# The down projection of one block pair as a Strassen level, summed in DRAM

## The chip, the cores and the metric

One core of a Trainium2 chip runs the whole kernel. The metric is the time of one execution on the device, in microseconds (us); of several runs the median counts.

## The reference

A transformer block on 2048 tokens of width D = 576, in float32: attention, then a gated feed-forward layer with F = 4608 hidden columns. Only the second half is touched here:

```
h   = x + attention(layernorm(x)) @ wo
n   = layernorm(h)
g   = n @ w_gate                  # 2048 x 4608
u   = n @ w_up
out = h + (sigmoid(g) * u) @ w_down   # w_down is 4608 x 576
```

## The kernel before

Tokens are split by parity and half into four blocks of 512 (`BLOCKS`), two to a pair: blocks 0 and 1 are pair 0, 2 and 3 pair 1. F is split into NF = 36 chunks of 128 hidden columns. The feed-forward part walks a list of items, one chunk for one block ("std") or for both blocks of a pair ("pair"):

```
items = ([("std", 0, f) for f in range(NSTD)] + [("pair", 0, f) for f in range(NSTD, NF)]
         + [("std", 1, f) for f in range(NSTD)] + [("pair", 1, f) for f in range(NF)])
```

While the first three runs of items go on, attention and output projection of later blocks run beside them (`bg_step`). The last run, 36 chunks of pair 1, has nothing beside it but its own down projection.

*Precision.* Each float32 operand of a matmul is split into a high part (ACT copies it into the format that TensorE reads) and a low part (DVE subtracts); this is `split`, lines L100 and L101. A product of two operands is then three matmuls: high x high, low x high, high x low.

*Gate and up* (`pair`). For a pair, gate and up are already one Strassen level over block, contraction half and gate/up: seven products `prod` (L532, six matmuls of 512 columns each), named b00, b10, t2, t3, t1, t4, b11 after their weights, and four small `rest` products (L539, two matmuls each) for the 64 left-over rows. That is 50 matmuls of 512 columns a chunk. They accumulate in three PSUM banks b1, b2, b3. ACT copies a running sum out of b1 between products (L588, L598, L605), DVE adds banks to these copies (L593, L606, L612), ACT takes the sigmoid, and DVE multiplies and splits the hidden tiles h0 and h1 (`hidden`, L545). Between the products stand the calls `side(i)`, i = 0 to 6, for background work.

*Weights.* SP loads chunk c + 2 (`load_gu`, L497: gate, up and down weights in one tile wg, two buffers) while chunk c is computed; `weights` forms the differences and splits, among them the 576 down columns into tile d.

*Down projection* (`down_units`). After every two chunks (a segment) one generator per block is put on a list, `queue`. Each of its four steps, called a unit, takes 128 tokens: 12 matmuls of 288 columns (L649: two chunks x three precision products x two column halves) into one of two PSUM tiles dp, then ACT copies 128x576 into the tile "stage" (L655). After the fourth unit POOL issues a DMA that adds the stage tile to the block's sum hacc[b] in DRAM (L659). `pair` calls `units(2)` at two places, after t1 and after b11, so two chunks give eight places for the eight units of a segment. hacc[b] was filled with h before. For blocks 2 and 3, the last two segments are added by DVE (L657) onto the sum read back by SP (L637), and SP writes the output (L663).

*Order.* The program is traced in this order, and a planner then orders each engine's instructions by priority (program order, with `high_priority` moving some ahead) and by the times that it expects: an instruction whose operands are not expected yet lets a later one go first. Each engine then runs its list strictly in order. Tiles of a pool share buffers; a new tile waits until all users of the old one are done.

Of the kernel before, what the change touches and what calls it, by code (L numbers as in the profile page):

```python
# [7 lines left out]

# [21 lines left out]
NS = 4  # L30
# [21 lines left out]
HI = 400  # L52
HC = 700
NSTD = 14


@with_exitstack
def kernel(ctx, tc, x, wqkv, wo, wmlp, out):
# [429 lines left out]
    st = ctx.enter_context(tc.tile_pool(name="st", bufs=2, reuse_waits="tile"))  # L488
# [6 lines left out]
    def load_gu(f, eng=sp):  # L495
        ws = gw.tile([P, WC], F32, bufs=2, name="wg")
        eng.dma_start(ws, wmlp[f])  # L497
        return ws

    def weights(kind, f, ws):  # L500
        with tc.high_priority(HI):
            wd = ws[:, GU:WC]
            r = ws[:, :GU].rearrange("p (c n) -> p c n", c=10)
            w1 = gw.tile([P, 2, 5, P], F32R, bufs=2, name="w1")
            split(w1[:, 0], w1[:, 1], r[:, 5:10])
            w4 = gw.tile([P, 2, 3, P], F32R, name="w4")
            w2 = gw.tile([P, 2, 4, P], F32R, name="w2")
            w3 = gw.tile([P, 8, P], F32R, name="w3").rearrange("p (a n) q -> p a n q", a=2)
            if kind == "std":
                split(w4[:, 0], w4[:, 1], r[:, 0:3])  # L510
                split(w2[:, 0, 0:2], w2[:, 1, 0:2], r[:, 3:5])
                ww = dict(b00=(w1, 0), b10=(w1, 2), b01=(w2, 0))
            else:
                t = gw.tile([P, 8, P], F32, name="tw")
                dve.tensor_tensor(t[:, 2:6], r[:, 1:5], r[:, 3:7], ALU.subtract)
                dve.tensor_tensor(t[:, 0:2], r[:, 1:3], t[:, 4:6], ALU.subtract)
# [6 lines left out]
        d = gd.tile([P, 2, D], F32R, bufs=4, name="d")  # L523
        split(d[:, 0], d[:, 1], wd)
        return ww, d

    def prod(ps, xx, w, n, first):
# [11 lines left out]
            pe.matmul(ps, wt[:, a, k0], xx[:, 4], start=False, stop=a == 1,  # L539
                      skip_group_check=True)  # L540

    def hidden(sg, ps, name):
        hh = gc.tile([P, TB], F32R, bufs=3, name=name + "h")
        hl = gc.tile([P, TB], F32R, bufs=3, name=name + "l")
        dve.tensor_tensor(sg, sg, ps, ALU.mult)  # L545
        split(hh, hl, sg)
        return hh, hl

    def s_tile():
        return gh.tile([P, TB], F32, tag="s", bufs=4, name="s")  # L550
# [29 lines left out]
        side(5)  # L580
        return {t: hid}

    def pair(X, w, units, side):
        b1, b2, b3 = b_tile(0), b_tile(1), b_tile(2)
        s1, s2, s3 = s_tile(), s_tile(), s_tile()
        prod(b1, X["a00"], w, "b00", True)
        with tc.high_priority(HC):
            act.activation(s1, b1, AF.Copy)  # L588
        side(0)
# [5 lines left out]
        side(1)  # L595
# [3 lines left out]
        side(2)  # L599
        prod(b3, X["s3"], w, "t3", True)  # L600
        side(3)
        prod(b1, X["s1"], w, "t1", False)
        rest(b1, X["a11"], w, "u4")
        with tc.high_priority(HC):
            act.activation(s3, b1, AF.Copy)  # L605
            dve.tensor_tensor(s3, s3, b3, ALU.add)  # L606
        units(2)
        side(4)
        prod(b3, X["a11"], w, "t4", False)
        rest(b3, X["a11"], w, "g4")  # L610
        with tc.high_priority(HC):
            dve.tensor_tensor(s2, s2, b3, ALU.add)  # L612
            act.activation(s2, s2, AF.Sigmoid)
        side(5)
        prod(b1, X["s4"], w, "b11", False)
        rest(b1, X["s4"], w, "u4")
        with tc.high_priority(HC):
            h0 = hidden(s1, b1, "h0")
            h1 = hidden(s2, s3, "h1")
        units(2)  # L620
        side(6)
        return {0: h0, 1: h1}

    tails = {}
    segs = [0] * 4
# [2 lines left out]
    def down_units(seg, b, t):  # L628
        e, hf = BLOCKS[b]
        left = NSEG - 1 - segs[b]  # L630
        segs[b] += 1
        add = b < 2 or left > 1
        if left != 0 or b < 2:
            hs = st.tile([P, NS, D], F32, name="stage")
            if not add:
                tails[b] = hs
                sp.dma_start(hs, hacc[b])  # L637
        else:
            hs = tails[b]
        for j in range(NS):  # L640
            js = slice(j * P, (j + 1) * P)
            ps = gp.tile([P, 2, 512], F32, bufs=2, name="dp")
            k = 0
            n = 3 * len(seg) - 1
            for hid, d in seg:
                hh, hl = hid[t]
                for a, m in ((hh, 0), (hl, 0), (hh, 1)):
                    for i in range(2):
                        pe.matmul(ps[:, i, :DH2], a[:, js], d[:, m, i * DH2:(i + 1) * DH2],  # L649
                                  start=k == 0, stop=k == n)  # L650
                    k += 1
            hv = hs[:, j].rearrange("p (i n) -> p i n", i=2)
            with tc.high_priority(HC):
                if add:
                    act.activation(hv, ps[:, :, :DH2], AF.Copy)  # L655
                else:
                    dve.tensor_tensor(hv, hv, ps[:, :, :DH2], ALU.add)  # L657
            if add and j == NS - 1:
                pool.dma_start(hacc[b], hs, accum_op=ALU.add, max_dma_last_dim=8 * D)  # L659
                if left == 0:  # L660
                    pool.dma_start(ov[e, hf], hacc[b])
            elif not add and left == 0:
                sp.dma_start(ov[e, hf][:, j], hs[:, j])  # L663
            yield


    def att_scr(at, blocks):
# [12 lines left out]
    def proj_scr(pj, b, raw, wos, wait):  # L680
# [10 lines left out]
        def tile_j(j, oj, hj):  # L691
            js = slice(j * P, (j + 1) * P)
            xj = []

            def put(pv, cs):
                if raw is None and not xj:
                    xj.append(pj.tile([P, 5, P], F32, bufs=2, name="xj"))
                act.activation(xj[0][:, cs] if raw is None else raw[:, cs, js], pv, AF.Copy)

            yield from proj_j(lambda: gp.tile([P, 512], F32, name="bgp"), oj, hj, wos,  # L700
                              th[:, :, js], tl[:, :, js], lambda: oj, put)
            act.dma_start(hacc[b][:, j], hj)
            if raw is None:
                act.dma_start(xscr[b][:, :, js], xj[0])

# [49 lines left out]
            yield from operands(pp, 0, X, ("s2", "s3", "s1", "a11", "s4"), a1)  # L755

    Xn = {}
    c = 0

    def under_rest(last_x):  # L760
# [18 lines left out]
        pp = ctx.enter_context(sb_pool("pp2", "right"))  # L779
        raw = yield from operands(pp, 1, Xn, ("s2", "s3", "s4"), a0)  # L780
        yield raw

# [40 lines left out]
    with tc.high_priority(2 * HI):  # L823
        wg = load_gu(0, pool)
        wg2 = load_gu(1, pool)
        wc = weights("std", 0, wg)
    wg = wg2
    seg = []

    def last_pair(i):  # L830
# [4 lines left out]
                X["a10"] = x_half(a10, None)  # L835
        bg_step(i)

    for c, (kind, p, f) in enumerate(items):
        w, d = wc
        skip = () if kind == "std" else (3,)  # L840
        if c == NSTD:
            finish_bg()
            last_x = splits[-1]
            bg = under_rest(getattr(last_x, "ins", last_x))
        if c == NF + NSTD:
            finish_bg()
            with tc.high_priority(HI):
                for n in ("s1", "a11"):
                    Xn[n] = x_half(*raw[n])
            X = Xn  # L850
        if c + 1 < len(items):
            wc = weights(items[c + 1][0], items[c + 1][2], wg)
        if c + 2 < len(items):
            wg = load_gu(items[c + 2][2])
        if kind == "std":
            hid = single(X, w, p, late, bg_step)
            blocks = [p]
        else:
            hid = pair(X, w, units, last_pair if c == NF - 1 else bg_step)
            blocks = [2 * p, 2 * p + 1]  # L860
        seg.append((hid, d))
        if len(seg) == 2:
            for b in blocks:
                queue.append(down_units(seg, b, b % 2))
            seg = []
# [44 lines left out]
```

## Time and profile before

| what | value |
|---|---|
| median of 3 runs | 1664.49 us (1664.44 to 1666.2) |
| profiled execution, its own time | 1665.37 us |
| its span in the profile | 1663.6 us, granted TensorE clock 0.981 |
| PE / DVE / ACT / POOL busy in the span | 96% / 68% / 49% / 6% |

PE is TensorE, PEld its loading of stationary operands, DVE VectorE, ACT ScalarE, POOL GpSimd, SP the engine that only issues DMAs. A group's row names the line of the code, the engine, the operation, out<-in with the names of tiles, the shape and the count; then busy us, mean ns, and idle time ahead with what ended it. A row of the timeline has start, duration, engine, line. Durations of matmuls overlap: their rate is read from starts.

### The profile page before, as it was taken

The numbers are of one execution on the slowest core, as the hardware profiler recorded it, in microseconds if no ns is written. First come the engines' busy times: TensorE is split into PE (matmuls) and PEld (weight loads), VectorE is DVE, ScalarE is ACT, GpSimd is POOL, SyncE is SP. The second block draws the span as 40 slices with busy tenths as digits, with TensorE's granted clock in tenths as the row PEclk, the third lists the DMA queues.
The fourth block names the chain that finished last, engine by engine and source line by source line (L and its number), as shares of the span: only waits on it lengthen the run. The fifth ranks groups of instructions, "written<-read, shape, count | busy, mean of one in ns | idle before, by whom it ended". The sixth has DMA issues, their size and how long they took to land.

```text
span 1663.6 us, 22174 instructions
## 1 busy us (share of the span) xinstructions
PE 1591.8 (96%) x8724; PEld 1416.3 (85%) x8724; DVE 1138.6 (68%) x1743; ACT 813.3 (49%) x1407; POOL 105.1 (6%) x114
## 2 busy tenths in 40 slices
PE   7899777999899999999899998999999999999999
PEld 6899776798788888888788897888888888888888
DVE  7999999456899999999444448644544545545544
ACT  5422224435555656655443446555555555555551
POOL 2000010000000000000000000000000000000000
PEclk9999988999999999999999999999999999999999
DMA  7447544757466676575957556365554455554562
GB/s 258 152 166 240 200 143 165 232 147 227 122 162 173 158 178 162 135 192 142 279 135 197 144 155 174 98 137 121 126 132 103 106 140 115 130 128 103 113 150 86
DMA packets 72392, 258.92 MB, mean 156 GB/s; under 512 B 8160, under 2 KB 20704, under 8 KB 71008
## 3 DMA queue, kind: packets, MB, share of 16 engines
q0 software_dynamic: 19328, 84.48, 26.8%
q1 hardware_dynamic: 32912, 143.60, 26.1%
q10 hardware_dynamic: 20048, 29.43, 4.8%
q8 instruction: 68, 1.11, 0.3%
q14 instruction: 36, 0.29, 0.1%
HBM read 145.42 MB, written 114.42 MB: 156 GB/s over the span
## 4 chain that ended last, share of the span: by engine, by line
PE 78%; DVE 9%; DMA 8%; ACT 2%; issue 1%; SPq 0%; POOL 0%; ACTq 0%; POOLq 0%; DVEq 0%
PE b L532 36%; PE dp L649 23%; PE acc L146 7%; PE b L539 7%; DMA wg<-in_wmlp_dram 5%; PE bgp L146 2%; DVE w L101 1%; DVE pr L194 1%; DMA o<-kw 1%; DVE pr L168 1%; DVE pr L199 1%; DVE lg L171 1%; DVE s L545 1%; PE acc L148 1%; PE acc L149 1%
## 5 line engine op out<-in xcount | busy, mean ns | idle before, releaser
L532 PE MATMUL b<-tl,w 128*128 128x512 f32 x1728 | 431.7, 395 | 18.0 <-ACT w L100 8.9
L532 PEld LDWEIGHTS b<-tl,w 128*128 128x128 f32 x1728 | 320.3, 190 | 82.3 <-ACT w L100 9.3
L532 PE MATMUL b<-th,w 128*128 128x512 f32 x1380 | 358.7, 395 | 4.4 <-DVE s L545 3.7
L532 PEld LDWEIGHTS b<-th,w 128*128 128x128 f32 x1380 | 256.0, 189 | 56.8 <-DVE s L545 4.0
L655 ACT ACTIVATE stage<-dp 128x576 f32<-128x576 f32 x272 | 175.9, 647 | 132.0 <-PE dp L649 128.7
L649 PE MATMUL dp<-d,h0h 128*128 128x288 f32 x1152 | 214.5, 297 | 4.9 <-ACT stage L655 4.9
L649 PE MATMUL dp<-d,h1h 128*128 128x288 f32 x1152 | 213.8, 296 | 0.0
L649 PEld LDWEIGHTS dp<-d,h0h 128*128 128x128 f32 x1152 | 179.5, 190 | 11.1 <-ACT stage L655 5.1
L649 PEld LDWEIGHTS dp<-d,h1h 128*128 128x128 f32 x1152 | 178.2, 189 | 5.6
L101 DVE TENSOR_TENSOR w<-wg,w 128x384 fp32r<-128x384 f32 (+2 forms) x200 | 129.0, 650 | 78.3 <-ACT w L100 78.2
L539 PE MATMUL b<-th,w 128*128 128x512 f32 x576 | 179.4, 393 | 0.0
L100 ACT ACTIVATE w<-wg 128x384 fp32r<-128x384 f32 (+2 forms) x200 | 117.8, 595 | 124.6 <-DMA wg<-in_wmlp_dram 50.9
L659 POOL DMA_DIRECT2D h<-stage x68 | 81.2, 1193 | 1189.4 <-ACT stage L655 1109.7
L146 PE MATMUL acc<-qw,th 128*128 128x432 f32 x512 | 155.9, 365 | 0.0
L101 DVE TENSOR_TENSOR w<-tw,w 128x512 fp32r<-128x512 f32 x116 | 79.8, 688 | 89.9 <-ACT w L100 89.7
L539 PEld LDWEIGHTS b<-th,w 128*128 128x128 f32 x576 | 109.4, 190 | 23.0
L612 DVE TENSOR_TENSOR s<-s,b 128x512 f32<-128x512 f32 x58 | 39.7, 685 | 126.2 <-PE b L539 126.2
L649 PE MATMUL dp<-d,h0l 128*128 128x288 f32 x576 | 124.9, 298 | 0.1
L649 PE MATMUL dp<-d,h1l 128*128 128x288 f32 x576 | 124.3, 297 | 0.0
L100 ACT ACTIVATE w<-tw 128x512 fp32r<-128x512 f32 x116 | 73.2, 631 | 88.5 <-PE b L532 84.6
L146 PEld LDWEIGHTS acc<-qw,th 128*128 128x128 f32 x512 | 98.5, 192 | 4.8 <-ACT th L100 0.3
L649 PEld LDWEIGHTS dp<-d,h0l 128*128 128x128 f32 x576 | 93.4, 190 | 0.6 <-DVE h0l L101 0.4
(185 smaller groups left out, 2075.1 us busy)
## 6 DMA issues: line engine op xcount, KB each, us to landing
h<-stage POOLq DMA_DIRECT2D x68, 1152.0 KB, 11.2
wg<-in_wmlp_dram SPq DMA_DIRECT2D x84, 928.0 KB, 5.4
kw<-k SPq DMA_DIRECT2D x16, 792.0 KB, 4.3
vw<-v SPq DMA_DIRECT2D x16, 792.0 KB, 4.6
h<-in_x_dram SPq DMA_DIRECT2D x20, 288.0 KB, 4.4
q<-ev ACTq DMA_DIRECT2D x16, 288.0 KB, 2.3
k<-ev ACTq DMA_DIRECT2D x16, 288.0 KB, 3.1
q<-q SPq DMA_DIRECT2D x16, 288.0 KB, 2.8
```

The costliest lines, as they stand in the source:

```text
L100: act.activation(hi, src, AF.Copy)
L101: splits.append(dve.tensor_tensor(lo, src, f32(hi), ALU.subtract))
L146: pe.matmul(ps[:, :n], a[:, c, js], m[:, c], start=k == 0, stop=False)
L148: pe.matmul(ps[:, :n], th[:, 4, js], wh[:, 4], start=False, stop=False)
L149: return pe.matmul(ps[:, :n], th[:, 4, js], wl[:, 4], start=False, stop=True)
L168: dve.tensor_tensor(pr[:, i], kw[:, j:j + W], q[:, j].unsqueeze(1).broadcast_to([P, W, CG]), ALU.mult)
L532: pe.matmul(ps, wt[:, a, k0 + c], xx[:, m + c], start=first and k == 0, stop=k == 5, skip_group_check=True)
L539: pe.matmul(ps, wt[:, a, k0], xx[:, 4], start=False, stop=a == 1, skip_group_check=True)
L612: dve.tensor_tensor(s2, s2, b3, ALU.add)
L649: pe.matmul(ps[:, i, :DH2], a[:, js], d[:, m, i * DH2:(i + 1) * DH2], start=k == 0, stop=k == n)
L655: act.activation(hv, ps[:, :, :DH2], AF.Copy)
L659: pool.dma_start(hacc[b], hs, accum_op=ALU.add, max_dma_last_dim=8 * D)
```

## The change

For the first 32 chunks of pair 1, the down projection takes two chunks (f even and odd), two blocks and two column halves of 288 as the three factors of a 2 x 2 x 2 product and does it as seven products instead of eight, in the form with running sums: hidden sums s1 to s4 (`seven`) and weight differences t1 to t4 (`down_side`). In detail:

- `down_seven` has 14 units: for each half u of 256 tokens, seven products k = 0 to 6 of six matmuls of 288 columns. Even products accumulate in one PSUM tile px, products 1 and then 3, 5 in py. After each, ACT copies the running sum to a tile "ev"; for every two products POOL adds it to one of seven sums in DRAM, `hsev`, that replaces hacc[2] and hacc[3].
- `pair` calls `between(i)` at seven places; in pair 1 each place takes one unit (in pair 0 two units at places 4 and 6, as before). Two chunks have 14 places.
- Down weights of pair 1 are loaded by themselves, two chunks at once (`load_down`), and split in `down_side`.
- A generator `lag(3)` puts three empty places ahead of the first `seven`.
- The residual h of blocks 2 and 3 is written to rows 0, 6, 2 and 4 of hsev; rows 1, 3 and 5 are filled with zeros by a memset tile z and two DMAs.
- The last NPL = 4 chunks stay with `down_units`. Ahead of them `load_tails` reads all seven sums back, adds three of them by DVE, and leaves five empty places.

```diff
-    hacc = [dr.tile([P, NS, D], F32, name=f"h{b}") for b in range(4)]
+    hacc = [dr.tile([P, NS, D], F32, name=f"h{b}") for b in range(2)]
+    hsev = dr.tile([P, 2, 7, 2, DH2], F32, name="h7")
...
+    def down_seven(ops):
+        for u in range(2):
+            for k, (a, m) in enumerate(ops):
+                if k == 0:
+                    px = gp.tile([P, 2, 512], F32, bufs=2, name="dp")
+                elif k in (1, 3):
+                    py = gp.tile([P, 2, 512], F32, bufs=2, name="dp")
+                ps = px if k % 2 == 0 else py
+                for i in range(2):
+                    js = slice((2 * u + i) * P, (2 * u + i + 1) * P)
+                    for q, (x, y) in enumerate(((0, 0), (1, 0), (0, 1))):
+                        pe.matmul(ps[:, i, :DH2], a[x][:, js], m[y],
+                                  start=k in (0, 1, 3) and q == 0, stop=q == 2,
+                                  skip_group_check=True)
+                if k % 2 == 0:
+                    hs = st.tile([P, 2, 2, DH2], F32, bufs=4, name="ev")
+                with tc.high_priority(HC):
+                    act.activation(hs[:, k % 2], ps[:, :, :DH2], AF.Copy)
+                if k % 2 or k == 6:
+                    k0 = k - k % 2
+                    pool.dma_start(hsev[:, u, k0:k + 1], hs[:, :k + 1 - k0], accum_op=ALU.add,
+                                   max_dma_last_dim=8 * D)
+                yield
...
+    def down_side(f, i):
+        if f % 2 == 0 and i == 0:
+            load_down(f)
+        t = M["wd"].rearrange("p c (h n) -> p c h n", h=2)
+        with tc.high_priority(HI):
...
+            elif f % 2:
+                if i == 0:
+                    d = dw.tile([P, 2, DH2], F32R, bufs=2, name="d3")
+                    split(d[:, 0], d[:, 1], t[:, 1, 1])
+                    M["b11"] = d[:, 0], d[:, 1]
+                    M["b00"], M["b10"] = pair_d(t[:, :, 0])
+                elif i == 4:
+                    dve.tensor_tensor(t[:, 0, 0], t[:, 0, 1], t[:, 0, 0], ALU.subtract)
+                    dve.tensor_tensor(t[:, 0, 1], t[:, 1, 1], t[:, 0, 1], ALU.subtract)
+                    dve.tensor_tensor(t[:, 1, 1], t[:, 1, 1], t[:, 0, 0], ALU.subtract)
+                    dve.tensor_tensor(t[:, 1, 0], t[:, 1, 0], t[:, 1, 1], ALU.subtract)
+                    M["t3"], M["t2"] = pair_d(t[:, :, 1])
+                elif i == 6:
+                    M["t1"], M["t4"] = pair_d(t[:, :, 0])
...
+    def seven():
+        r00, r01, r10, r11 = (R[n] for n in ("00", "01", "10", "11"))
+        sx = dk.tile([P, TB], F32, name="sx")
+        with tc.high_priority(HI):
+            dve.tensor_tensor(sx, r10, r11, ALU.add)
+            dve.tensor_tensor(r10, r00, r10, ALU.subtract)
+            dve.tensor_tensor(r00, sx, r00, ALU.subtract)
+            s2 = sum_halves("s2", r00)
+            s3 = sum_halves("s3", r10)
+            s1 = sum_halves("s1", sx)
+            a11 = halves("h1", r11)
+            dve.tensor_tensor(r01, r01, r00, ALU.subtract)
+            s4 = sum_halves("s4", r01)
+        return down_seven(((M["a00"], M["b00"]), (M["a01"], M["b10"]), (s2, M["t2"]),
+                           (s3, M["t3"]), (s1, M["t1"]), (a11, M["t4"]), (s4, M["b11"])))
...
+    def load_tails():
+        nonlocal st
+        dk_stk.close()
+        st_stk.close()
+        st = st_stk.enter_context(sb_pool("st3"))
+        dz = ctx.enter_context(sb_pool("dz", "right"))
+        for b, rows in ((2, ((0, 1), (6, None))), (3, ((2, 5), (4, 3)))):
+            hs = tails[b] = st.tile([P, 2, 2, 2 * DH2], F32, name=f"tail{b}")
+            for h, (k, k2) in enumerate(rows):
+                sp.dma_start(hs[:, h], hsev[:, :, k].rearrange("p u i n -> p u (i n)"))
+                if k2 is not None:
+                    h2 = dz.tile([P, 2, 2 * DH2], F32, name=f"more{b}{h}")
+                    sp.dma_start(h2, hsev[:, :, k2].rearrange("p u i n -> p u (i n)"))
+                    dve.tensor_tensor(hs[:, h], hs[:, h], h2, ALU.add)
+        yield from lag(5)
...
+            def between(i):
+                units(1)
+                down_side(f, i)
```

More of the change, by code (lines that the diff above doesn't have):

```diff
@@ L54 @@
 NSTD = 14
+NPL = 4
+LAG = 3
 @with_exitstack
@@ L522, in weights @@
             ww.update(g4=(w1, 4), u4=(w4, 0), b11=(w4, 1))
-        d = gd.tile([P, 2, D], F32R, bufs=4, name="d")
-        split(d[:, 0], d[:, 1], wd)
+        d = None
+        if down:
+            d = d_tile()
+            split(d[:, 0], d[:, 1], wd)
         return ww, d
@@ L581, in single, with pair @@
         return {t: hid}
-    def pair(X, w, units, side):
+    def pair(X, w, between, last):
         b1, b2, b3 = b_tile(0), b_tile(1), b_tile(2)
@@ L606, in pair @@
             dve.tensor_tensor(s3, s3, b3, ALU.add)
-        units(2)
-        side(4)
+        between(4)
         prod(b3, X["a11"], w, "t4", False)
@@ L617, in pair @@
         with tc.high_priority(HC):
[L618 to L622, printed above, removed]
+            last((s1, b1), (s2, s3))
+        between(6)
     tails = {}
@@ L632, in down_units @@
         add = b < 2 or left > 1
-        if left != 0 or b < 2:
+        if add:
             hs = st.tile([P, NS, D], F32, name="stage")
-            if not add:
-                tails[b] = hs
-                sp.dma_start(hs, hacc[b])
         else:
@@ L778, in under_rest @@
             yield from proj_scr(pj, 3, None, wos, 5)
-        pp = ctx.enter_context(sb_pool("pp2", "right"))
+        z = st.tile([P, NS, D], F32, name="stage")
+        pool.memset(z, 0.0)
+        for u in range(2):
+            act.dma_start(hsev[:, u, 1:6:2], z[:, 0:3].rearrange("p k (i n) -> p k i n", i=2))
+        pp = pp_stk.enter_context(sb_pool("pp2", "right"))
         raw = yield from operands(pp, 1, Xn, ("s2", "s3", "s4"), a0)
@@ new lines, in hid_raw, with sum_halves, last_sums, last @@
+    def hid_raw(name, sg, ps):
+        R[name] = r = dk.tile([P, TB], F32, name="r" + name)
+        dve.tensor_tensor(r, sg, ps, ALU.mult)
+        return r
+    def sum_halves(name, src):
+        hh = dk.tile([P, TB], F32R, name=name + "h")
+        hl = dk.tile([P, TB], F32R, name=name + "l")
+        split(hh, hl, src)
+        return hh, hl
+    def last_sums(f):
+        def last(h0, h1):
+            if f % 2 == 0:
+                M["a00"] = halves("h0", hid_raw("00", *h0))
+                hid_raw("10", *h1)
+            else:
+                M["a01"] = halves("h0", hid_raw("01", *h0))
+                hid_raw("11", *h1)
+        return last
@@ new lines, in lag @@
+    def lag(n):
+        for _ in range(n):
+            yield
+    def load_tails():
[13 more added lines that the diff above has]
+        yield from lag(5)
@@ L850, with last, between @@
             X = Xn
+            pp_stk.close()
+            dw = ctx.enter_context(sb_pool("dw", "right"))
+            dk = dk_stk.enter_context(sb_pool("dk", "right"))
+        if c == NF + NSTD + 1:
+            st_stk.close()
+            st = st_stk.enter_context(sb_pool("st2"))
         if c + 1 < len(items):
-            wc = weights(items[c + 1][0], items[c + 1][2], wg)
+            wc = weights(items[c + 1][0], wg, c + 1 < NF + NSTD)
         if c + 2 < len(items):
-            wg = load_gu(items[c + 2][2])
+            wg = load_gu(items[c + 2][2], n=WC if c + 2 < NF + NSTD else GU)
+        hid = {}
+        blocks = [p] if kind == "std" else [2 * p, 2 * p + 1]
+        def last(h0, h1):
+            hid[0] = hidden(*h0, "h0")
+            hid[1] = hidden(*h1, "h1")
         if kind == "std":
             hid = single(X, w, p, late, bg_step)
-            blocks = [p]
-        else:
-            hid = pair(X, w, units, last_pair if c == NF - 1 else bg_step)
-            blocks = [2 * p, 2 * p + 1]
+        elif not by_seven:
+            side = last_pair if c == NF - 1 else bg_step
+            def between(i):
+                if i in (4, 6):
+                    units(2)
+                side(i)
+            pair(X, w, between, last)
+        else:
+            def between(i):
+                units(1)
+                down_side(f, i)
+            pair(X, w, between, last if f >= NF - NPL else last_sums(f))
+            if f < NF - NPL:
+                if f % 2:
+                    if f == 1:
+                        queue.append(lag(LAG))
+                    queue.append(seven())
+                    for b in blocks:
+                        segs[b] += 1
+                continue
+            d = M[f]
         seg.append((hid, d))
         if len(seg) == 2:
+            if by_seven and not tails:
+                tails.update({2: None, 3: None})
+                queue.append(load_tails())
             for b in blocks:
```

60 lines of the change are left out of this document (44 added, 16 removed).

## The prediction

> **What bounds the kernel now.** I read the page first (busy shares, slices, chain), then the table by stage, then TensorE's instructions over one chunk of the stage that changes, then the groups of VectorE and ScalarE there, then the DMA queues.
>
> ```profile
> PE 1591.8 (96%) x8724; PEld 1416.3 (85%) x8724; DVE 1138.6 (68%) x1743; ACT 813.3 (49%) x1407; POOL 105.1 (6%) x114
> PE 78%; DVE 9%; DMA 8%; ACT 2%; issue 1%; SPq 0%; POOL 0%; ACTq 0%; POOLq 0%; DVEq 0%
> 450.00:800.00 350.00, 350.00 (x1921) 309.37 (x1920) 339.56 (x459) 208.71 (x338) 22.65 (x19) 1.00 0.64 162
> 1100.00:1600.00 500.00, 500.00 (x2760) 443.60 (x2759) 253.44 (x421) 270.59 (x451) 33.38 (x28) 1.00 0.54 121
> ```
>
> The last two rows are stretches of time: length, then busy us of PE, PE's weight loads, DVE, ACT and POOL, granted clock, DMA share. The second of them lies inside the stage that the change rewrites (pair 1, blocks 2 and 3, from about 1032 us to the end). There PE is never idle, at full clock, while DVE is 51% and ACT 54% busy. So a matmul taken out of this stage is worth its issue time, as long as nothing else becomes late.
>
> TensorE over one chunk:
>
> ```profile
> 1611.13 1.54 PE L532 MATMUL b<-tl,w 128*128 128x512 f32 x6
> 1612.52 1.52 PE L532 MATMUL b<-th,w 128*128 128x512 f32 x6
> ...
> 1618.41 0.62 PE L539 MATMUL b<-th,w 128*128 128x512 f32 x2
> 1618.86 0.42 PE L649 MATMUL dp<-d,h0h 128*128 128x288 f32 x2
> ...
> 1622.05 1.54 PE L532 MATMUL b<-th,w 128*128 128x512 f32 x6
> ...
> 1628.88 1.54 PE L532 MATMUL b<-tl,w 128*128 128x512 f32 x6
> ```
>
> A chunk takes 1628.88 - 1611.13 = 17.75 us. Two down units, 24 matmuls of 288 columns, lie between 1618.86 and 1622.05: 3.19 us, 0.133 us each (the durations in the rows overlap; starts give the rate). Four units are 6.38 us, and the 50 matmuls of 512 columns have the other 11.37 us, 0.227 us each. 50 x 0.227 + 48 x 0.133 = 17.75, so there is no gap in it, and the stage cannot get faster except by fewer matmuls.
>
> **The change part by part.** All of it is in pair 1; its first 32 chunks, taken as 16 twos of 35.5 us, are done by the seven products.
>
> *Matmuls removed.* Two chunks and two blocks now cost 8 units of 12, 96 matmuls of 288 columns; then 7 products x 2 halves x 6, 84 of the same shape, with as many weight loads. 12 x 0.133 = 1.60 us a two, x 16 = **-25.5 us**. A two then takes 33.9 us. The last four chunks and blocks 0 and 1 keep their units.
>
> *More evictions, splits and sums.*
>
> ```profile
> L655 ACT ACTIVATE stage<-dp 128x576 f32<-128x576 f32 x124 | 80.3, 648 | 66.3 <-PE dp L649 64.8
> L101 DVE TENSOR_TENSOR d<-wg,d 128x576 fp32r<-128x576 f32 x30 | 22.6, 753 | 0.0
> L101 DVE TENSOR_TENSOR h0l<-s,h0h 128x512 fp32r<-128x512 f32 x31 | 21.3, 688 | 0.0
> L100 ACT ACTIVATE d<-wg 128x576 fp32r<-128x576 f32 x30 | 20.1, 671 | 0.0
> L100 ACT ACTIVATE h0h<-s 128x512 fp32r<-128x512 f32 x31 | 19.6, 634 | 9.8 <-DVE s L545 9.8
> L516 DVE TENSOR_TENSOR tw<-wg,tw 128x256 f32<-128x256 f32 x32 | 13.5, 423 | 0.6
> ```
>
> A two has 14 evictions of 128x576 on ACT instead of 8: 6 x 0.648 = 3.9 us. Seven hidden operands are split instead of four: 3 x 0.634 = 1.9 on ACT and 3 x 0.688 = 2.1 on DVE. Four sums of 128x512 come on DVE, 4 x 0.688 = 2.8. The down weights are split as three of 576 and one of 288 columns instead of two of 576: about 0.671 + 0.45 = 1.1 on ACT, 0.753 + 0.45 = 1.2 on DVE (0.45 my estimate for 288 columns, a little over the 0.423 of 256), and four subtractions of 288, 1.8, on DVE. Of ACT that makes 270.59/500 x 35.5 = 19.2, + 6.9 = 26.1 of 33.9 us (77%); of DVE 18.0 + 7.8 = 25.8 (76%). I cost all this at nothing as load, because between 450 and 800 us DVE was 97% busy under a PE that lost nothing. It counts only as lateness, next.
>
> *Cover that becomes thinner.* Now each chunk puts two units (3.19 us) between the product s1 and the product t4, which writes the bank b3 that ACT (L605) and DVE (L606) must first have finished with, and two more before the next chunk. Then one seven unit, 0.80 us, stands at each of seven places. What happens with no cover is seen at the first two chunks of this stage, where the queue of units runs nearly dry:
>
> ```profile
> 1032.42:1045.37 12.95, 12.95 (x58) 10.35 (x58) 9.29 (x16) 7.30 (x14) 0.72 (x1) 1.00 0.67 202
> PEld b L532 <- ACT s L605: 0.5, 2, 0.3
> PEld b L532 <- ACT s L588: 0.4, 2, 0.2
> PEld b L532 <- DVE s L606: 0.4, 2, 0.2
> PEld b L532 <- DVE s L612: 0.3, 1, 0.3
> ```
>
> The period holds 50 + 7 matmuls, 12.3 us by the rates above, and takes 12.95: 0.65 us lost, in four small waits of the weight loads. It is that little because the planner pulls other products forward. So a chunk of the new stage loses between 0 (as with two units) and 0.65 us (as with none); 32 chunks, 0 to 21 us. One unit nearly spans the 0.60 us copy and its hand-over, so I take 0.15 a chunk, **+5 us**. Less than nothing is excluded, since the old chunk has no gap. The places without units (the lag of 3 at the start, the 5 empty steps of load_tails) are 8 of such places, where a chunk has 7: bounds 0 and 0.75 us, I take **+0.5**.
>
> *Accumulation in DRAM.* Per two, 14 x 288 KB = 4.13 MB go to the seven sums instead of 2.36 MB to h, in 8 issues instead of 2.
>
> ```profile
> q0 software_dynamic: 7737, 33.59, 35.9%
> q1 hardware_dynamic: 4032, 26.61, 17.5%
> h<-stage POOLq DMA_DIRECT2D x28, 1152.0 KB, 10.7
> L659 POOL DMA_DIRECT2D h<-stage x28: 1184/1192/1209, 1115.7 to 1594.5; - x28
> ```
>
> These rows are of 1100 to 1600 us. 28 accumulations took 35.9% of 500 us, 6.4 us of all sixteen engines each; 14/4 of one is 22.4 us a two. The 28 loads took 17.5%, 3.1 us each, 6.3 a two. Together 28.7 of 33.9 us, 85% instead of 54%. POOL's issues are at most 8 x 1.19 = 9.5 us of 33.9 and only accumulations queue behind them. An eviction buffer is wanted again six units, some 14 us, after its DMA is issued, against 10.7 us to landing at twice the size. I cost this at nothing; if the packets were dearer, the evictions would stop, and PE after them (the second rival). The first weighing of a page: for a DMA issued from POOL the Trainium skill ("DMA: Bandwidth & Descriptors", Anatomy of one DMA — SWDGE (gpsimd) path) gives about 2.0 us + bytes/436e3. By it 1152 KB would land in an estimated 4.7 us, and that rival would have no chance; the trace's 10.7 us speaks against using it for these accumulations.
>
> On SP one load a two of the down weights is added and each other load is shorter; they wait for buffers freed one chunk ahead. The zeros (a memset on POOL, two writes) and the residuals written into rows of the seven sums fall in the stage before, where they take one of two staging buffers for about the 5 us of a plain 1152 KB transfer; bounds 0 and 5, I take 0, since the two buffers alternate and one is filled while the other drains.
>
> *The end.* The last four chunks add onto sums read back from DRAM.
>
> ```profile
> 1603.49 18.53 SPq L637 DMA_DIRECT2D stage<-h  x2
> 1620.64 0.75 DVE L657 TENSOR_TENSOR stage<-stage,dp 128x576 f32<-128x576 f32 x1 [0.20 <-DMA h<-stage]
> stage<-h SPq DMA_DIRECT2D x2, 1152.0 KB, 5.3
> h<-stage POOLq DMA_DIRECT2D x1, 1152.0 KB, 9.0
> out_dram<-stage SPq DMA_DIRECT2D x8, 288.0 KB, 2.1
> ```
>
> Now the load comes in time: DVE waited 0.20 us. Then the last seven unit runs in chunk 34 after its third product. Until the third down unit, which needs a bank that a DVE add has emptied, PE has 30 matmuls of chunk 34 (6.8 us), 26 of chunk 35 (5.9) and two units of 1.6: 15.9 us. Against it: the eviction 0.65, the issue 1.2, the accumulation (2.1 for 288 KB plain, 9.0 for 1152 KB), and the loads of seven rows, 4.0 MB (5.3 for the one that is wanted first, 18.5 for all queued): 9 to 29 us. So PE waits 0 to 13 us; I take **+2**, nearer the lower rows, as only the last row is 288 KB late and the others can be read before it. The final ten units are without a gap either way, and what follows the last matmul (4.1 us) stays.
>
> *Sum*, against the profiled execution's own 1665.4 us (span 1663.6 and 1.8 around it): -25.5 + 5 + 0.5 + 2 = -18, 1647.4. That execution lies 0.9 above the median shown, 1664.5, so I predict 1646.5 us.
>
> **Rivals.**
> *The cover is lost (about 1662 us).* Every chunk loses the 0.65 us of an uncovered one: +21 instead of +5. For it: the chain after s1 needs 1.6 us (0.60 on ACT, 0.69 on DVE, hand-overs) and the unit gives 0.80. Against: only four waits of 0.2 to 0.3 us were left even with nothing. It would be no change by measurement, which here tells 0.2%, 3.3 us.
>
> *DMA becomes the bound (about 1684 us).* A two needs 28.7 us of the DMA engines; if accumulations cost 1.3 times as much in smaller pieces, it needs 22.4 x 1.3 + 6.3 = 35.4, and all is lost; above that the kernel is slower. For it: 85% already by the rows, and landings in the trace reach 15.1 us, 1.41 times the median.
>
> ```profile
> DMA to landing us min/median/max: 8.7/11.2/15.1
> ```
>
> With 1.41 a two takes 37.9, +2.4 x 16 = 38 us, 1703; halfway from break-even, 1684. Against: pieces of 4.6 KB a partition are near the mean packet of q0, 33.59 MB/7737 = 4.3 KB.
>
> *The tail waits (about 1656 us).* All seven rows must land before the first add: 10 us more than I took. A pause as long as that also costs clock:
>
> ```profile
> 1011.63 2.01 PE L532 MATMUL b<-th,w 128*128 128x512 f32 x6 [3.74 <-DVE s L545]
> ```
>
> After 3.74 us without matmuls, six took 2.01 instead of 1.52 us; a microsecond in all until it recovers. Second page: the Trainium skill ("TensorE: Matmul & The Clock Gate", Part 1) says an idle window of about 3.4 us halves the clock until about as long a busy one; the trace agrees in kind, so a wait of ten would become about eleven and a half, an estimate from that page, and 1656 about 1657.
>
> *The count does not fall.* The loops give 84 plainly; 1 in 100.
>
> **How the numbers follow.** Forecast (losses of 0 to 16 us, 1639 to 1655): 0.70. Cover lost: 0.09, of it 0.05 within 0.2%. Tail: 0.09, of it 0.02 within 0.2% (the whole 13 us with cover partly lost). DMA: 0.11, slower. No fewer matmuls: 0.01, same. Faster by over 0.2% 0.70 + 0.04 + 0.07 = 0.81, within 0.08, slower 0.11. The range reaches down to 1638 (all losses nothing) and up to 1661, taking in the tail and part of the lost cover; the DMA case and the worst of the others stay out, some 0.19.
>
> **What would show it.** Right: 192 fewer matmuls of 288 columns; a two of 34 to 34.3 us between equal products; PE near 100% from 1100 us on with DVE and ACT near 76%; DMA share near 0.85; accumulations landing in under 11 us. Wrong: PE waiting for evictions and these for DMA buffers (second rival); waits of b's weight loads for L605 or L606 in every chunk above 0.3 us (first); a pause above 3 us ahead of the last units with DVE waiting for the tails (third).

## The result, and the profile after

The changed kernel takes 1709.39 us (median of 4 runs, 1705.46 to 1712.97) against 1665.35 for the kernel before beside it: ratio 1.0268, 95% interval 1.0249 to 1.0287. It is slower by 44 us where 18 us less was forecast. The profiled execution took 1708.49 us (span 1706.6, granted clock 0.972).

The page, busy times, and then the table by stage (stretch, length, busy us of PE, its weight loads, DVE, ACT and POOL, granted clock, DMA share, GB/s):

```profile
PE 1592.5 (93%) x8532; PEld 1398.5 (82%) x8532; DVE 1253.6 (73%) x1954; ACT 897.8 (53%) x1583; POOL 178.0 (10%) x211
```

```profile
1000.00:1100.00 100.00, 87.80 (x433) 73.18 (x432) 76.54 (x125) 62.34 (x108) 10.87 (x13) 0.95 0.71 172
1100.00:1600.00 500.00, 470.33 (x2437) 402.14 (x2437) 329.28 (x566) 322.60 (x567) 91.07 (x107) 0.98 0.80 160
1600.00:1706.00 106.00, 96.89 (x537) 85.04 (x535) 59.81 (x91) 44.73 (x77) 10.22 (x12) 0.97 0.63 151
```

8724 - 8532 = 192 matmuls are gone, as the change says. But between 1100 and 1600 us PE, never idle before, is idle for 29.7 us and runs at clock 0.98. Neither DVE (66%) nor ACT (65%) is near full there, and DMA is at 0.80.

How long a two now takes comes from one tile: s4 is the last product of each half u, so its matmuls run from the first half of the first two to the second half of the sixteenth, 15.5 twos.

```profile
L688 PE MATMUL dp<-d,s4h x128: 291/293/298, 1067.8 to 1651.4; 128*128 128x288 f32 x128
```

583.6 us, less the unit itself (0.66 us from its first matmul to its last), by 15.5 is 37.6 us a two, against 33.9 forecast without a loss: 3.7 x 16 = 59 us lost. The waits between 1100 and 1600 us (us in total, times, longest) say where:

```profile
ACT d L104 <- DMA wd<-in_wmlp_dram: 40.0, 13, 5.3
DVE d L105 <- ACT d L104: 38.0, 26, 4.4
...
PEld dp L688 <- ACT ev L694: 24.4, 13, 4.1
...
PE dp L688 <- ACT ev L694: 21.4, 13, 3.8
...
PEld b L542 <- DVE s L619: 15.2, 26, 1.1
```

Thirteen times, once a two, ACT waits some 3 us for the down weights, and PE 1.6 us on average (0.65 to 3.84) for an eviction by ACT. One of these stops, in the timeline of SP, ACT and PE (start, duration, engine, line; in brackets the idle time ahead and what ended it):

```profile
1236.29 0.38 SPq L891 DMA_DIRECT2D wd<-in_wmlp_dram  x1
...
1239.98 0.65 ACT L694 ACTIVATE ev<-dp 128x576 f32<-128x576 f32 x1
...
1241.77 0.29 PE L688 MATMUL dp<-d,h0h 128*128 128x288 f32 x1
...
1244.41 0.29 PE L688 MATMUL dp<-d,h0h 128*128 128x288 f32 x1
...
1245.90 1.02 ACT L104 ACTIVATE d<-wd 128x288 fp32r<-128x288 f32 x2 [5.27 <-DMA wd<-in_wmlp_dram]
...
1246.82 0.61 ACT L104 ACTIVATE w<-tw 128x512 fp32r<-128x512 f32 x1
...
1247.34 0.61 ACT L104 ACTIVATE s4h<-r 128x512 fp32r<-128x512 f32 x1
...
1247.86 0.63 ACT L694 ACTIVATE ev<-dp 128x576 f32<-128x576 f32 x1
...
1248.54 0.61 PE L688 MATMUL dp<-d,s2h 128*128 128x288 f32 x1 [3.84 <-ACT ev L694]
...
1250.15 3.35 PE L542 MATMUL b<-th,w 128*128 128x512 f32 x7
```

SP reloads the single wd buffer at 1236.29. The first split of it stands in ACT's list right behind an eviction that ends at 1240.63; the data come so late that it starts at 1245.90. ACT stands 5.27 us in front of it. The next eviction, of the half's first product, has its last matmul at 1241.77 but runs at 1247.86, since ACT takes its list in order. PE, in order too, does the second product, the last of it at 1244.41, and then has s2h, which goes on in the bank that this eviction must first have read. PE stops for 3.84 us, and then seven matmuls of 512 columns take 3.35 us instead of 1.6.

On the order, the Trainium skill ("TensorE: Matmul & The Clock Gate", Part 1, Architectural detail) calls ACT's and DVE's queues strict first-in, first-out, and the trace agrees.

The granted clock is 0.50 from 1247 us until after 1253. Of the thirteen stops for an eviction, all four of 2.70 to 3.84 us were followed by a clock of 0.50, and none of the nine of at most 1.51 us was. On this the same page of the Trainium skill (Part 1, What's actually happening) gives an idle window of about 3.4 us for the drop to half. The stop of 3.84 us, with 0.48 us per matmul after it, agrees; those of 2.70, 2.99 and 3.02 us were shorter and cost the clock too (the first and the last with a second stop of some 0.75 us behind them), so the figure is no safe limit here.

The DMA view of the same 500 us (queues: packets, MB, share; issues: KB each, median us to landing):

```profile
q0 software_dynamic: 15151, 54.41, 61.2%
q1 hardware_dynamic: 7424, 25.36, 18.7%
...
h<-ev POOLq DMA_DIRECT2D x80, 576.0 KB, 6.9
wg<-in_wmlp_dram SPq DMA_DIRECT2D x27, 640.0 KB, 4.9
h<-ev POOLq DMA_DIRECT2D x27, 288.0 KB, 6.1
wd<-in_wmlp_dram SPq DMA_DIRECT2D x13, 576.0 KB, 7.1
```

The accumulations land in 6.9 us and hold nobody up; it is the plain load of wd that takes 7.1. The mean share of 0.80 hides how full the DMA engines are while this load is under way. In the stop above, from its issue to its first use and then until 1250 us, the share is 1.02 and 0.12 (second number from the right):

```profile
1236.30:1245.90 9.60, 8.41 (x47) 7.22 (x45) 5.54 (x10) 3.69 (x7) 1.71 (x2) 1.00 1.02 251
1245.90:1250.00 4.10, 1.46 (x6) 1.46 (x7) 2.96 (x6) 3.61 (x7) 0.19 (x1) 0.60 0.12 21
```

Two smaller losses, PE at the two ends of the stage:

```profile
1016.48 0.85 PE L655 MATMUL dp<-d,h1h 128*128 128x288 f32 x2 [9.58 <-ACT h1h L104]
```

```profile
1672.38 0.85 PE L655 MATMUL dp<-d,h0h 128*128 128x288 f32 x2 [4.46 <-DVE tail L664]
```

At the start the pause of 3.74 us of before has become 9.58 (+5.8); the tail, which had none, has 4.46. With 59 that makes 69, less 25.5 for the matmuls: +44, against 43.1 measured between the two profiled executions.

At the start, too, ACT stands in front of a load. It waits 9.30 us for the gate and up weights (4.00 in the kernel before), and the split h1h that PE needs comes behind them in its list, at 1015.81:

```profile
1013.29 0.74 ACT L104 ACTIVATE w<-wg 128x640 fp32r<-128x640 f32 x1 [9.30 <-DMA wg<-in_wmlp_dram]
```

### The profile page after: what moved, and what is told of

Its sections match the earlier page's. It is cut to its first block, busy times and chain, and to the rows that moved or that the text cites. A ratio compares the mean times of both kernels' runs of the same rounds, so it can differ in the third digit from the quotient of the medians.

```text
span 1706.6 us, 22466 instructions
## 1 busy us (share of the span) xinstructions
PE 1592.5 (93%) x8532; PEld 1398.5 (82%) x8532; DVE 1253.6 (73%) x1954; ACT 897.8 (53%) x1583; POOL 178.0 (10%) x211
## 5 line engine op out<-in xcount | busy, mean ns | idle before, releaser
L694 ACT ACTIVATE ev<-dp 128x576 f32<-128x576 f32 x224 | 144.8, 647 | 32.7 <-PE dp L688 25.7
L697 POOL DMA_DIRECT2D h<-ev x128 | 109.1, 852 | 504.3 <-ACT ev L694 494.9
L655 PE MATMUL dp<-d,h0h 128*128 128x288 f32 x640 | 122.4, 301 | 9.4 <-ACT stage L662 4.9
L655 PE MATMUL dp<-d,h1h 128*128 128x288 f32 x640 | 120.8, 298 | 9.6 <-ACT h1h L104 9.6
L662 ACT ACTIVATE stage<-dp 128x576 f32<-128x576 f32 x144 | 93.0, 646 | 67.3 <-PE dp L655 65.0
L655 PEld LDWEIGHTS dp<-d,h0h 128*128 128x128 f32 x640 | 101.7, 194 | 13.5 <-ACT stage L662 5.2
L655 PEld LDWEIGHTS dp<-d,h1h 128*128 128x128 f32 x640 | 99.9, 191 | 13.1 <-ACT h1h L104 9.8
L666 POOL DMA_DIRECT2D h<-stage x36 | 43.0, 1195 | 638.5 <-ACT stage L662 576.4
L150 PE MATMUL acc<-qw,tl 128*128 128x432 f32 x256 | 93.8, 367 | 0.0
L172 DVE TENSOR_TENSOR pr<-kw,q 128x1152 f32<-128x1152 f32 x64 | 85.2, 1353 | 4.5 <-DMA kw<-k 3.8
## 6 DMA issues: line engine op xcount, KB each, us to landing
h<-stage POOLq DMA_DIRECT2D x36, 1152.0 KB, 11.2
```

What stands on the lines that cost most here:

```text
L150: pe.matmul(ps[:, :n], a[:, c, js], m[:, c], start=k == 0, stop=False)
L172: dve.tensor_tensor(pr[:, i], kw[:, j:j + W], q[:, j].unsqueeze(1).broadcast_to([P, W, CG]), ALU.mult)
L694: act.activation(hs[:, k % 2], ps[:, :, :DH2], AF.Copy)
L697: pool.dma_start(hsev[:, u, k0:k + 1], hs[:, :k + 1 - k0], accum_op=ALU.add, max_dma_last_dim=8 * D)
```

## Experiments

Theory: ACT's place in front of a load that lands late makes nearly all of the loss. The rivals: too little cover between the products (the waits for L619), DMA engines too full whatever the order, and the writes of zeros. Each ratio is to runs of the kernel before on the same chip; between chips, ratios compare better than times.

**The splits of wd at ordinary priority.**

```diff
-        with tc.high_priority(HI):
+        with tc.high_priority(0):
```

> Only change to the changed kernel: the splits and differences of the down weights (down_side) are traced at ordinary priority instead of HI. Theory W (ACT stands at the head of its queue waiting for the load wd, because the planner puts the split right where it expects that load to land, and evictions and then PE wait behind it): the 40 us of ACT waits for wd between 1100 and 1600 us and the 24 us of waits of L688's weight loads for L694 go to nearly nothing, the clock there goes back to 1.00, and the time falls by about 30 us, from 1709 to about 1680. Theory D (the 16 DMA engines are too full, whatever the order): the same bytes move, so the time stays within 5 us of 1709. Theory C (cover too thin at place 4): stays, too.

Measured: 1726.1 us, ratio 1.0375 (1.0337 to 1.0414). Slower still, and the wait stayed:

```profile
ACT d L104 <- DMA wd<-in_wmlp_dram: 40.6, 13, 4.2
```

The edit didn't remove what it was meant to remove. The reload is released by the last split of the old weights, and with that split later, it came later too: issued at 1242.98, and the first split of the new weights ran at 1250.44, again after a wait (3.99 us). A lower priority orders an instruction only among those that the planner takes to be ready; it does not keep an early one from an engine with a free place. So this run says nothing against the theory, but neither for it.

**The zeros some 500 us earlier** (memset and two writes moved to the start of `under_rest`).

> Only change to the changed kernel: the zero tile and its two writes into rows 1, 3, 5 of the seven sums are traced at the start of the second run of items (pair 0), some 500 us earlier. Theory Z (the two writes of 884 KB at about 1000 us delay the loads of wg and x there, and PE's pause of 9.6 us at 1016 us, 3.7 before, is theirs): the pause goes back to about 4 us, time 5 to 7 us less than 1709. If the pause has another cause: within 2 us of 1709.

Measured: 1706.97 us, ratio 1.0244 (1.02 to 1.0287) against 1.0268 (1.0249 to 1.0287): not clear of the scatter. PE's pause at the start fell from 9.58 to 6.38 us, but it also began later and ended at 1018.35 instead of 1016.48 us.

**More cover where PE waits for L619.**

```diff
-                units(1)
+                units((1, 0, 1, 1, 2, 0, 2)[i])
```

> Only change to the changed kernel: the seven units of a chunk stand as 1, 0, 1, 1, 2, 0, 2 at places 0 to 6 instead of one at each, so that two stand after the product s1 as in the kernel before. Theory C (the waits of b's weight loads for L619, 18 us in all, come from the thin cover at place 4): these waits fall below 5 us and the time by 10 to 15 us, to about 1696. Theory W: the waits for L619 are followed ones, of chunks that were already late; the time changes by less than 5 us.

Measured: 1715.88 us, ratio 1.0293 (1.0256 to 1.033). No gain, and the waits for L619 did not fall (PEld 16.4 us, PE 12.0; 15.2 and 8.2 without the edit). More cover alone removes neither.

**All three together.**

> The three edits together (splits of the down weights at ordinary priority, zeros early, units 1, 0, 1, 1, 2, 0, 2). If W, Z and C all hold and add: 1709 - 30 - 6 - 12, about 1661, still some 20 us above the 1640 that PE's work alone gives, of which the tail (4.5 us pause and its slow clock) is 6. If D holds: not below 1700.

Measured: 1712.02 us, ratio 1.0278 (1.0242 to 1.0314), ACT's wait for wd 41.4 us. PE no longer waits for evictions there, but 35.3 us in all for a DVE product (L925) that stands behind DVE's part of the same splits. None of the three touches the cause.

**The splits held back on ACT.** An edge in the order puts them behind ACT's copy of a sum (L601 or L618) in the same chunk; buffers, DMAs and arithmetic are unchanged.

```diff
+            MK["a"] = act.activation(s1, b1, AF.Copy)
...
-        with tc.high_priority(HI):
+        mk = MK["a"]
+        with tc.high_priority(HI), tc.issue_after(getattr(mk, "ins", mk)):
```

> Only change to the changed kernel: an ordering edge. The splits of the down weights are queued on ACT behind ACT's copy s1 (place 0) or s3 (place 4) of the chunk that traces them, so that ACT reaches them a chunk after their load was issued. Theory W: ACT's waits for wd between 1100 and 1600 us fall from 40 us to under 5, the waits of L688's weight loads for L694 from 24 us to under 5, the clock returns to 1.00, and the time falls by 25 to 35 us, to about 1680. Theory D (too much DMA work): the same bytes move, the waits turn up at other operands; time above 1700.

Measured: 1668.04 us, ratio 1.0027 (1.0014 to 1.0039): 41 us of the 44 are gone. Table by stage, DMA and waits, 1100 to 1600 us:

```profile
1100.00:1600.00 500.00, 499.99 (x2644) 430.83 (x2644) 356.56 (x612) 352.97 (x616) 98.49 (x116) 1.00 0.87 174
```

```profile
wd<-in_wmlp_dram SPq DMA_DIRECT2D x14, 576.0 KB, 6.6
```

```profile
PEld b L542 <- DVE s L621: 5.4, 29, 0.2
```

PE is full, at clock 1.00, with DMA at 0.87 instead of 0.80; wd still takes 6.6 us to land, but no wait for it, nor of PE for an eviction, is left. So the DMA engines don't bind PE once nobody stands in front of the load, and the waits of L621 (L619 before the edit) fell from 15.2 to 5.4 us by themselves: they were a consequence.

**Half of the accumulations left out** (the sums of products 2 to 5 are never added, so those terms are missing; no edge).

```diff
-                if k % 2 or k == 6:
+                if k in (1, 6):
```

> The changed kernel without the additions of rows 2 to 5 to DRAM (two of four DMAs of each half; the sums in these rows stay at their starting values): 1.8 MB instead of 4.1 MB for two chunks, less than the 2.4 MB of the kernel before. Order and work of the engines are otherwise the same. Theory D: with the load of the DMA engines back under that of before, nearly all of the loss in the stage goes: 1650 to 1665. Theory W: wd lands in about 5 us instead of 7, so that ACT's wait falls from 3 us a two to 1: about 1690.

Measured: 1657.79 us, ratio 0.9958 (0.9943 to 0.9972).

```profile
1100.00:1600.00 500.00, 499.99 (x2664) 433.90 (x2663) 355.35 (x611) 356.29 (x620) 49.44 (x58) 1.00 0.52 107
```

```profile
wd<-in_wmlp_dram SPq DMA_DIRECT2D x15, 576.0 KB, 4.0
```

With DMA at 0.52 the load lands in 4.0 us and ACT's wait is gone without any edit of the order. In the stop shown above, a landing in 4.0 us would have been at 1240.3, just before ACT was free. In the stretch where this run's load is under way (1220.7 to 1224.8 us) the DMA share is 0.64, not 1.02. The same cause from the other side: the accumulations hurt by making another load late.

**The edge, with half of the accumulations left out.**

> Both: the ordering edge, and no additions of rows 2 to 5. Theory W: no better than the ordering edge alone by more than 5 us, since with the wait gone the DMA load does not matter. Theory D: as without the rows alone, and well below the ordering edge alone. What is left above 1640 in this kernel is the start of the stage, the end and the thinner cover: I expect 1655.

Measured: 1662.59 us, ratio 0.998 (0.9965 to 0.9996), 5 us under the edge alone. Once nobody stands in front of wd, halving the accumulations is worth 5 us, not 50, and none of it lies in the stage: s4's matmuls span 540.5 us in both runs with the edge. What is gone is a pause of 3.29 us in the tail; the rest lies ahead of the stage in the two traces and isn't explained. It is also 5 us over the run without the edge, where s4's matmuls span 537.0 us: the edge itself costs 3.5 us in the stage.

**The edge, with the zeros early.**

> The ordering edge, and the zeros written early. Theory Z: 4 us less than the ordering edge alone.

Measured: 1666.08 us, ratio 1.0011 (0.9995 to 1.0026), 2 us less than the edge alone, with intervals that overlap. PE's pause at the start is shorter:

```profile
1021.33 0.85 PE L657 MATMUL dp<-d,h1h 128*128 128x288 f32 x2 [6.20 <-ACT h1h L104]
```

6.20 us instead of 9.26 with the edge alone, and ACT's wait for wg in front of it is 5.08 instead of 8.98. So the zeros were one part of that wait. But as with the zeros early alone, the pause ends later in this trace (1021.33 instead of 1019.53 us): PE comes to it some 5 us later. That the shorter pause makes the 2 us isn't shown.

**Two buffers for wd**, loaded two chunks ahead; no edge. For the room, ev has three buffers instead of four and the split sums a pool that opens a chunk later.

```diff
-        M["wd"] = t = dw.tile([P, 2, D], F32, name="wd")
+        W2[f] = t = dw.tile([P, 2, D], F32, bufs=2, name="wd")
...
-            load_down(f)
+            if f == 0:
+                load_down(0)
+            if f + 2 < NF:
+                load_down(f + 2)
+            M["wd"] = W2[f]
```

> The changed kernel with the load wd issued two chunks earlier into a second buffer (paid for with three eviction buffers instead of four, and the sum tiles allocated a chunk later); no ordering edge, the same DMA traffic. Theory W, a second way of taking the wait away: ACT's waits for wd go below 5 us between 1100 and 1600, PE's waits for L694 with them, time about 1665, like the ordering edge. If the edge helped by something else (the order of ACT around it): above 1690. If three eviction buffers are too few: new waits of ACT's L694 for DMA.

Measured: 1660.79 us, ratio 0.9974 (0.9958 to 0.999): under the kernel before, with the same DMA traffic and no wait for wd.

```profile
1100.00:1600.00 500.00, 499.99 (x2666) 433.96 (x2666) 357.00 (x612) 356.53 (x622) 99.09 (x116) 1.00 0.87 175
```

```profile
L688 PE MATMUL dp<-d,s4h x128: 291/293/297, 1067.3 to 1603.9; 128*128 128x288 f32 x128
```

A two takes (536.6 - 0.66)/15.5 = 34.6 us. While a load of wd is under way the DMA share is 1.04 here too (1220.7 to 1227.5 us), and PE is full. Three eviction buffers are a little few: ACT waits 11.0 us in 500 for one to come free, at most 1.2 at a time, and PE for none of it. What is left is the start (the 9.26 us pause) and the tail, PE and DVE:

```profile
1623.96 0.53 PE L655 MATMUL dp<-d,h0h 128*128 128x288 f32 x2 [3.52 <-DVE tail L664]
```

```profile
1621.88 1.36 DVE L982 TENSOR_TENSOR tail<-tail,more 128x1152 f32<-128x1152 f32 x1 [4.34 <-DMA more<-h]
```

**Eight empty places ahead of the last units instead of five** (`lag(8)`), with early zeros, over two buffers and over the edge.

> Two wd buffers, zeros early, and eight empty places instead of five before the last down units. The pause of PE ahead of them (4.5 us in the changed kernel, with slow matmuls behind) goes to under 1 us: 4 to 5 us; the zeros 2; with the wait for wd gone 1658, less than the 1665 of the kernel before. If the tails' reads only move with it: 1663.

> The ordering edge, zeros early, and eight empty places: 1666 - 4, about 1662; the chunk stays at 17.4 us.

Measured: 1663.28 us, ratio 0.9977 (0.9963 to 0.9991), and 1665.62 us, ratio 0.9993 (0.998 to 1.0006). Empty places didn't remove the tail's wait, and the first of the two runs is 2.5 us over the two buffers alone (the intervals overlap). In it DVE stands at the same line (4.12 us), and now PE's products stand behind it:

```profile
1628.61 2.93 PE L542 MATMUL b<-th,w 128*128 128x512 f32 x6 [4.12 <-DVE s L619]
```

**Two buffers, and block 3's sums behind block 2's adds on DVE.** In the tail DVE stood in front of L982 for a late row of block 3, ahead of the adds of block 2 that free PE's banks: the stage's pattern once more.

```diff
-                    dve.tensor_tensor(hs[:, h], hs[:, h], h2, ALU.add)
+                    if b == 2:
+                        dve.tensor_tensor(hs[:, h], hs[:, h], h2, ALU.add)
+                    else:
+                        pend.append((hs[:, h], h2))
...
+            if b == 3 and pend:
+                with tc.issue_after(LT["a"]):
+                    for y, z in pend:
+                        dve.tensor_tensor(y, y, z, ALU.add)
```

> As e14_two_buffers (1660.8, ratio 0.9974 to before), with one more edit: the two sums of block 3's rows are put behind the last add of block 2's first down units in VectorE's order, so that VectorE no longer stands waiting for the late row of block 3 ahead of the adds that free TensorE's banks. If that place in the order is what makes the tail's pause of 3.5 us, the pause falls to the wait for block 2's own row, and the time to 1656 to 1658 (ratio about 0.995). If the rows themselves are late whatever the order, the pause only moves to block 3's units: 1660 to 1661. The main stage should read as in e14: 34.5 us per two chunks, no wait for wd.

Measured: 1656.06 us, ratio 0.994 (0.9924 to 0.9957), the fastest here with the whole computation. DVE in the tail:

```profile
1617.31 1.36 DVE L993 TENSOR_TENSOR tail<-tail,more 128x1152 f32<-128x1152 f32 x1
1619.97 1.42 DVE L671 TENSOR_TENSOR tail<-tail,dp 128x576 f32<-128x576 f32 x2 [1.30 <-DMA tail<-h]
...
1627.27 1.35 DVE L651 TENSOR_TENSOR tail<-tail,more 128x1152 f32<-128x1152 f32 x1
1628.60 0.69 DVE L624 TENSOR_TENSOR s<-s,b 128x512 f32<-128x512 f32 x1
1629.20 1.35 DVE L651 TENSOR_TENSOR tail<-tail,more 128x1152 f32<-128x1152 f32 x1
```

No wait of PE for DVE above 0.2 us is left there; the two sums of block 3 (L651) run without waiting. So the order on DVE makes the pause. But as in the stage it takes a late row besides: with half of the accumulations left out, and the old order, DVE waited at most 0.46 us for a row, and PE had no pause in the tail.

## Why the prediction was wrong

**The matmuls removed: right.** 192 fewer.

**The step that failed** is the sentence on SP: one load of the down weights a two is added, and the loads "wait for buffers freed one chunk ahead". It was costed at nothing, and nobody was named who would stand in front of it. The term that should have stood there is some 48 us. wd has one buffer, freed by the last split of the old weights, and the first split of the new ones is put on ACT at once. The price was about 3 us a two (37.6 against 34.6), 48 us in all; the two-buffer run shows it (1709 to 1661). 2.2 of the 3 is PE idle, for evictions and for L619 (29.7 us in 500, which are 13.3 twos); the rest goes with the slower clock after the stops (0.02 of 500 us is 0.75 us a two). The prediction did ask what queues behind POOL's issues, but not what queues behind the first use of this load.

**"Nothing as load", DVE and ACT at 76% and 77%: right for load, beside the point for order.** In the two-buffer run they are 71% and 71% busy under a full PE. ACT was the culprit at 65%: not busy, but standing.

**Accumulation in DRAM.** 85% of DMA time was forecast, 0.87 measured in the runs with a full PE: the sum was right, and on the mean nothing is bound by it. The rival that DMA becomes the bound held the right sign and a part of the mechanism. Its sign of being wrong, PE waiting for evictions, came true, but these waited for the split ahead of them in ACT's list and not for DMA buffers. Its price was misread: 15.1 us is the longest landing of an accumulation in the whole kernel before, and beside the median in the same row, 11.2, it is 1.35 times and not 1.41 (36.5 us a two and not 37.9). What neither had is that a mean of 0.80 or 0.87 has stretches of 7 to 10 us at 1.0 in it, and that a load which falls into a full stretch comes late: 7.1 us for wd, against 4.0 in the run with a mean of 0.52.

**Cover made thinner: mis-sized.** +5 us was taken; with the wait gone a two takes 34.6 us instead of 33.9, 0.7 x 16 = 11 us, within the bounds of 0 to 21. Only a part of it is cover: the waits of PE's weight loads for L619 are 3.0 us in 500, 0.2 us a two. In one chunk of the two-buffer run (1302.39 to 1319.76 us) the seven products take 9.89 us by their starts, against 9.56 in a chunk of the kernel before (from 1302.61). Five take 1.38 or 1.39 us, as a product right behind matmuls of 288 columns did before (1.36 behind matmuls of 512); two take 1.47 and 1.49. So breaking the stage up at seven places instead of two has a price in issue time as well, for which the sum had no term. How the 11 us divide exactly isn't shown.

**Zeros and the start: mis-sized.** 0 was taken. The pause at the start grew by 5.8 us, with ACT waiting for wg. The two writes of zeros, 864 KB each, landed in 10.2 us beside it; without them there the pause is 3 us shorter, but no gain in time is shown. What makes the rest stays open; it isn't the load of wd, which is first issued at 1029.1 us.

**The tail: mis-sized.** +2 was taken, 0 to 13 as bounds; a pause of 4.46 us was there, and of 3.3 to 3.5 in the edge and two-buffer runs with five empty places. The rival that the tail waits named this sign, a pause above 3 us with DVE waiting for the tails, but gave as its reason that all seven rows must land before the first add. They need not: a DVE add for block 3 was put ahead of those for block 2.

**With the waits out of the way**, the prediction's own sum comes out with these sizes put in. Of the last run's profiled execution, 1655.0: 1665.4 - 25.5 + 10.2 (34.54 us a two) + 5.8 (its pause at the start is 9.57 us) + 0 (tail) = 1655.9.

## What to carry to other kernels

An engine that runs its list in order is no cheap place for the first use of a load: ask of every new load how late it may land, which engine's list has its first reader, and what stands behind that reader. A second buffer, or the reader put behind work that has to be done anyway, was worth 41 to 49 us here with the traffic unchanged. Where an engine is two thirds busy and another waits for it, look first for what it stands in front of.

## What was not expected of the hardware

A mean DMA share below 1 does not say that a load finds the DMA engines free. In the changed kernel and the runs with the edge or two buffers, with means of 0.80 to 0.88 over 500 us, the load of wd (576 KB) took 6.6 to 7.1 us at the median and 9.6 at worst; where looked at, the share was 1.0 while it was under way. With a mean of 0.52, and 0.64 while it was under way, it took 4.0. PE ran full in all of them but the changed kernel, where ACT stood in front of the load.

The second is how short a stop can cost clock. After a stop of 2.99 us the granted clock was 0.50, and in the run with more cover even after three short ones, of 0.90, 0.27 and 0.95 us within 3.7 us (0.50 from 1131 to 1134 us). The stage had a clock of 0.98 over 500 us with the stops, and 1.00 without them.
